# A shorter substitution completed by TensorE products, and two products of the chain formed ahead of it

## The chip, the cores and the metric

The kernel runs on one core of a Trainium2 chip. The metric is the device time of one execution in microseconds. Most executions of a kernel agree to within a per cent, and each is given a state, fast or slow, by its distance from the fastest of the same kernel. Where two kernels are compared, the executions alternate on the same chip.

## The reference

The delta rule is run as a recurrence over 768 positions for 4 batches and 8 heads of size 48. A Fourier mixing block and an MLP with float64 weights follow (code shortened).

```python
def _attn_ref(q, k, v, beta):                       # B, H, S, D = 4, 8, 768, 48
    k_n = k / (np.linalg.norm(k, axis=-1, keepdims=True) + 1e-06)
    state = np.zeros((B, H, D, D))
    for t in range(S):
        y[:, :, t] = einsum('bhd,bhde->bhe', q[:, :, t], state)
        v_old = einsum('bhde,bhd->bhe', state, k_n[:, :, t])
        state = state + beta_t * einsum('bhd,bhe->bhde', k_n[:, :, t], v[:, :, t] - v_old)
def _moe_ref(x, w_ch1, w_ch2):                      # x: 4 x 768 x 384; w: 384 x 1536, 1536 x 384
    mixed = real(fft(fft(x, axis=1), axis=2))
    u = x + mixed
    un = (u - mean(u)) / sqrt(var(u) + 1e-06)
    return u + maximum(un @ w_ch1, 0) @ w_ch2
```

## The kernel before

The recurrence is worked in chunks of 64 positions (12 per batch). Each chunk needs the inverse T of a triangular 64x64 matrix. Six groups of eight chunks each form these inverses. A chunk's matrix is split into quarters of 32: VectorE inverts the two diagonal ones of all heads at once by substitution, and TensorE completes the inverse with the products `pj`.

```python
def mm(o, lhsT, rhs, start, stop=True):
    nc.tensor.matmul(o, lhsT=lhsT, rhs=rhs, start=start, stop=stop, skip_group_check=True)

def invert(g):                                        # W = 32, QT = 4
    A = grams.pop(g)
    X = wk.tile([128, W, W], F32, tag="X", name="X")
    nc.vector.transpose(X..., A[:, :, :, 0]...)
    # ... norms, scaling by beta, mask Y on GpSimd ...
    for j in range(1, W - 1):                         # 30 steps, two VectorE operations each
        n = W - 1 - j
        t = A...[:, 0:j, 0, 0:n]
        nc.vector.tensor_tensor(t, X[:, j:j + 1, j + 1:]..., X[:, 0:j, j:j + 1]..., op=ALU.mult)
        nc.vector.tensor_tensor(X[:, 0:j, j + 1:], X[:, 0:j, j + 1:], t, op=ALU.add)
        yield
    # ...
    Z = wk.tile([128, 2 * QT, 4, W], F32, tag="X", name="Z")   # shares its buffer with X
    nc.vector.transpose(Z..., Y...)
    nc.vector.transpose(A[:, :, :, 0]..., Y...)
    for lh in range(2):                               # half groups
        for step in range(2):
            pj = ps_pair("pj", "pair")...
            # ... 32 products of 32x32 (c, u, hh) into pj, then 4 ScalarE copies into A, wt ...
            yield

def chain(m):                                         # one chunk of one batch, in series
    # pk: 8 products of the keys KQT with the state
    nc.vector.tensor_tensor(R, V4[:, c], pk, op=ALU.subtract)
    # pu: 8 products of R with wt (that is T)
    nc.scalar.activation(U, pu, ACT.Copy)
    # pS: 8 products of kp with U; VectorE adds them to the state
    later.append(outputs(...))                        # py: read by ScalarE into x

# order of the program (shortened)
run(keys(0)); run(keys(1))
first = invert(0)
advance(first, 4)
run(both(first, seq(keys(2, 3), queries(0, 1))))
scaled(0)
pre = both(invert(1), queries(2, 3))
for m in range(STEPS):
    # chain steps, between which pre is advanced, and behind pre the weights' conversion:
    # if m < 2 * QT and not advance(pre): advance(side)
    # from batch 1 on the MLP of the batch before runs beside the chain
```

An fp32 product counts as two passes of TensorE in the trace, each with a weight load of its own.

## Time and profile before

| | before |
|---|---|
| median of 4 executions | 830.9 us (828.5 to 840.1) |
| span of the profiled one | 832.2 us |
| TensorE (PE) busy | 740.3 us, 8024 passes |
| VectorE (DVE) busy | 397.8 us |
| ScalarE (ACT) busy | 286.4 us |
| first transposes of the MLP of batch 0 | 198.7 us |

The slices, the busy time by stretch and the timeline of before stand in the prediction below.

### The profile page before, as it was taken

To read this page: it belongs to the slowest core of one execution; us is meant where nothing else is said; L and a number is where in the kernel's file an instruction comes from. 1 tells how busy PE (TensorE), PEld (TensorE's weight loads), DVE (VectorE), ACT (ScalarE), POOL (GpSimd) and SP (SyncE) were. 2 spreads that over 40 slices of the span, in tenths; PEclk is the share of its full clock that TensorE was granted. 3 is DMA by queue.
4 is the path that set the end of the run, shared out by engine and by line. 5 is a ranking of instruction groups with operands and counts; after the bars stand their busy time and mean duration, and the time that the engine had idled before them with its cause. 6 is when DMAs were issued, how large, how long until landed. Compare 5 with 4: busy or idle time off the path is not lost.

```text
span 832.2 us, 18790 instructions
## 1 busy us (share of the span) xinstructions
PE 740.3 (89%) x8024; PEld 549.2 (66%) x8024; DVE 397.8 (48%) x1036; ACT 286.4 (34%) x667; POOL 45.8 (6%) x67
## 2 busy tenths in 40 slices
PE   4768777795999987899999899999899989999997
PEld 3537666674767665675766766766667667676784
DVE  5986959859931148951169313499110124210000
ACT  5725268541272142451431632511511112030120
POOL 3000000011000000010000001000000010000000
PEclk9995955587999998969999799999699999999999
DMA  7542326510111121001111001001000000000000
GB/s 159 123 96 44 61 48 219 151 25 6 25 35 23 35 41 27 14 11 35 29 19 45 2 11 30 1 2 39 2 1 20 2 20 1 9 10 20 9 10 19
DMA packets 84051, 30.81 MB, mean 37 GB/s; under 512 B 79248, under 2 KB 80784, under 8 KB 83968
## 3 DMA queue, kind: packets, MB, share of 16 engines
q1 hardware_dynamic: 80880, 26.63, 14.3%
q0 software_dynamic: 912, 2.59, 0.9%
q8 instruction: 63, 1.03, 0.5%
q10 hardware_dynamic: 2176, 0.39, 0.3%
q14 instruction: 20, 0.16, 0.1%
HBM read 24.87 MB, written 4.72 MB: 36 GB/s over the span
## 4 chain that ended last, share of the span: by engine, by line
PE 64%; DVE 16%; ACT 10%; issue 3%; DMA 3%; SPq 2%; POOL 1%; POOLq 0%; DVEq 0%; ACTq 0%
PE ph L124 20%; PE po L124 19%; PE pc L124 6%; PE py L124 5%; PE pg L124 3%; DVE X L465 3%; PE pf L124 3%; DVE A L463 3%; PE pj L124 2%; PE pb L124 2%; PE pt L127 2%; ACT A L407 2%; SPq L156 1%; ACT wt L497 1%; ACT wt L500 1%
## 5 line engine op out<-in xcount | busy, mean ns | idle before, releaser
L124 PE MATMUL ph<-unT,w 128*128 128x256 f32 x864 | 221.7, 405 | 6.2 <-ACT hT L723 2.9
L124 PE MATMUL po<-w,hT 128*128 128x384 f32 x576 | 200.3, 495 | 0.0
L124 PEld LDWEIGHTS ph<-unT,w 128*128 128x128 f32 x864 | 164.0, 198 | 37.2 <-ACT hT L723 6.1
L124 PEld LDWEIGHTS po<-w,hT 128*128 128x128 f32 x576 | 105.1, 190 | 65.3 <-issue 0.5
L723 ACT ACTIVATE hT<-ph 128x256 f32<-128x256 f32 x144 | 55.0, 383 | 207.9 <-PE ph L124 207.6
L563 DVE TENSOR_TENSOR st<-st,pc 48x192 f32<-48x192 f32 x88 | 30.9, 351 | 96.3 <-PE pc L124 62.7
L736 DVE TENSOR_TENSOR x<-x,po 128x384 f32<-128x384 f32 x24 | 13.3, 554 | 126.6 <-PE po L124 126.5
L546 ACT ACTIVATE U<-pc 128x192 f32<-128x192 f32 x48 | 15.8, 330 | 120.9 <-PE pc L124 111.8
L124 PE MATMUL pc<-R,wt 64*64 64x48 f32 x768 | 41.6, 246 | 13.1 <-DVE R L537 7.2
L124 PEld LDWEIGHTS pc<-R,wt 64*64 64x64 f32 x768 | 33.6, 156 | 28.9 <-DVE R L537 9.1
L463 DVE TENSOR_TENSOR A<-X 128x30 f32<-128x30 f32 (+9 forms) x150 | 50.5, 337 | 3.8
L465 DVE TENSOR_TENSOR X<-X,A 128x30 f32<-128x30 f32 (+9 forms) x150 | 49.2, 328 | 3.7
L124 PE MATMUL py<-st,KQT 128*64 128x96 f32 x352 | 45.9, 280 | 0.8 <-ACT x L583 0.6
L407 ACT ACTIVATE A<-pg 32x256 f32<-32x256 f32 x108 | 36.6, 369 | 19.3 <-PE pg L124 18.7
L124 PE MATMUL pg<-KQT 48*64 48x128 f32 (+1 forms) x896 | 36.7, 311 | 6.3 <-ACT w L407 2.3
L124 PE MATMUL py<-U,LQ 64*64 64x48 f32 x768 | 40.7, 240 | 0.0
L124 PEld LDWEIGHTS pg<-KQT 48*64 48x64 f32 x896 | 28.5, 177 | 17.2 <-ACT KQT L374 4.7
L124 PEld LDWEIGHTS py<-st,KQT 128*64 128x64 f32 x352 | 35.7, 155 | 5.8 <-issue 1.9
L124 PE MATMUL pf<-stab,scr 128*128 128x128 f32 (+6 forms) x192 | 28.1, 299 | 9.1 <-DVE scr L634 9.0
L124 PEld LDWEIGHTS py<-U,LQ 64*64 64x64 f32 x768 | 34.7, 154 | 2.2 <-issue 1.2
L660 DVE TENSOR_TENSOR x<-x,pb 128x193 f32<-128x193 f32 (+1 forms) x96 | 27.1, 346 | 18.3 <-PE pb L124 18.3
L124 PEld LDWEIGHTS pf<-stab,scr 128*128 128x128 f32 (+2 forms) x192 | 25.9, 193 | 13.5 <-DVE scr L634 6.4
(127 smaller groups left out, 807.2 us busy)
## 6 DMA issues: line engine op xcount, KB each, us to landing
w<-in_moe_w_ch_dram SPq DMA_DIRECT2D x12, 768.0 KB, 4.6
qp<-in_q_dram SPq DMA_DIRECT2D x96, 48.0 KB, 2.4
V<-in_v_dram SPq DMA_DIRECT2D x96, 48.0 KB, 2.4
kp<-in_k_dram SPq DMA_DIRECT2D x88, 48.0 KB, 2.4
out_dram<-x SPq DMA_DIRECT2D x8, 192.0 KB, 1.9
out_dram<-x SPq DMA_DIRECT2D x4, 168.0 KB, 2.1
stab<-k_stab SPq DMA_DIRECT2D x1, 640.5 KB, 4.7
kp<-in_k_dram ACTq DMA_DIRECT2D x8, 48.0 KB, 3.4
```

The lines of the kernel that those rows point to most:

```text
L124: nc.tensor.matmul(o, lhsT=lhsT, rhs=rhs, start=start, stop=stop, skip_group_check=True)
L127: nc.tensor.matmul(o, lhsT=src, rhs=ident[0:src.shape[0], 0:src.shape[0]], is_transpose=True, start=start, stop=True, skip_group_check=True)
L156: engs[hh].dma_start(out=dst[64 * hh:64 * hh + CH, c, :, 0:D], in_=src[b, 4 * hh:4 * hh + 4, t0:t0 + CH, :].rearrange("h p d -> p h d"))
L407: nc.scalar.activation(ce(A[pr, ns, :, sl]), src, ACT.Copy)
L463: nc.vector.tensor_tensor(t, X[:, j:j + 1, j + 1:].broadcast_to([128, j, n]), X[:, 0:j, j:j + 1].broadcast_to([128, j, n]), op=ALU.mult)
L465: nc.vector.tensor_tensor(X[:, 0:j, j + 1:], X[:, 0:j, j + 1:], t, op=ALU.add)
L497: nc.scalar.activation(wt[r1, :, :, 0:W], Z[r1, ns], ACT.Copy)
L546: nc.scalar.activation(U, pu, ACT.Copy)
L563: nc.vector.tensor_tensor(nst[pr, :, :, e, :], st[pr, :, :, e, :], pS[pr], op=ALU.add)
L660: nc.vector.tensor_tensor(dst, dst, src, op=op)
L723: nc.scalar.activation(hT[:, fc, :], ph, ACT.Relu)
L736: nc.vector.tensor_tensor(x[:, T, :], x[:, T, :], po, op=ALU.add)
```

## The change

Three things are done for the first groups or the first batch, to get the MLP started sooner (they touch groups 0 and 1, the chain of batch 0 and the front). In groups 0 and 1 VectorE substitutes over blocks of 16 instead of 32, 14 steps instead of 30. TensorE joins the blocks by products `pe` and `pz` over all four quarters. For the first batch the chain uses T B K and T B V, formed ahead of it (`pm`, `pv`), so each step of the chain loses a product and a copy. And in the front the constants are fetched first, while the products that transpose beta move behind the first keys.

```diff
+    pack = const.tile(...); bt = ...; k0 = ...; v0 = ...        # all four fetched here, ahead of the memsets
+    nc.gpsimd.dma_start(out=pack, in_=cn["pack"].ap())
...
     def invert(g):
+        narrow = g < 2
...
-        for j in range(1, W - 1):
+        for j in range(1, (H if narrow else W) - 1):            # H = 16
+            if narrow:
+                n = H - 1 - j
+                t = ts[:, :, 0:j * n].rearrange("p h (s t) -> p h s t", t=n)
+                nc.vector.tensor_tensor(t, XB[:, :, j:j + 1, j + 1:]..., XB[:, :, 0:j, j:j + 1]..., op=ALU.mult)
+                nc.vector.tensor_tensor(XB[:, :, 0:j, j + 1:], XB[:, :, 0:j, j + 1:], t, op=ALU.add)
...
         for lh in range(2):
+            if narrow:
+                quarters = [(slice(W * i, W * i + W), c, u) for c in range(QT) for u in range(4) for i in range(4)]
+                pe = ps_one([128, QT, 4, W], "pe")
+                mm(pe..., ident, eyes[:, None, :]..., True)
+                for r, c, u in quarters:
+                    mm(pe[r, c, u], A[r, QT * lh + c, u, 0], Z[r, QT * lh + c, u], False)
+                nc.scalar.activation(E[:, lh], pe, ACT.Copy)
+                pz = ps_pair("pz", "pair")...
+                for r, c, u in quarters:
+                    mm(pz[r, 0, c, u], AD[r, QT * lh + c, u], E[r, lh, c, u], c == 0 and u == 0)
+                for r, c, u in quarters:
+                    mm(pz[r, 1, c, u], E[r, lh, c, u], AD[r, QT * lh + c, u], c == 0 and u == 0)
+                nc.scalar.activation(Z[:, ns], pz[:, 0], ACT.Copy)
+                nc.scalar.activation(A[:, ns, :, 0], pz[:, 1], ACT.Copy)
...
+    def combined(m):                       # 8 products pm into KQT, 8 products pv into the values, one copy each
...
-        pu = ...; U = ...                  # for every chunk
+        if m < NCH: U = R                  # first batch: neither products nor copy
...
     run(keys(0))
+    betas()                                # was ahead of the first keys
...
-    scaled(0)
+    combined(0); combined(1)
```

## The prediction

> **What bounds the kernel now.** I read first the busy shares in 40 slices (20.8 us each, tenths).
>
> ```profile
> PE   4768777795999987899999899999899989999997
> DVE  5986959859931148951169313499110124210000
> PEclk9995955587999998969999799999699999999999
> ```
>
> From slice 10 (about 200 us) to the end TensorE (PE) is at 9 nearly everywhere; before that VectorE (DVE) is the fuller engine. So there are two stages: a preparation, and a long stretch bound by PE. The busy time by stretch sizes them (columns: PE, weight loads, DVE, ScalarE, GpSimd busy us with counts, granted clock, DMA share, GB/s).
>
> ```profile
> 26.30:62.30 36.00, 24.14 (x296) 16.32 (x296) 31.86 (x89) 15.96 (x48) 0.00 (x0) 0.97 0.48 95
> 62.30:71.30 9.00, 6.29 (x198) 5.79 (x200) 2.51 (x2) 7.39 (x13) 1.85 (x1) 0.50 0.34 58
> 71.30:113.00 41.70, 33.56 (x730) 28.25 (x730) 36.02 (x95) 11.08 (x26) 0.00 (x0) 0.75 0.27 48
> 121.80:163.40 41.60, 30.50 (x570) 26.93 (x565) 36.82 (x92) 31.69 (x72) 0.00 (x0) 0.54 0.65 191
> 163.40:198.70 35.30, 24.02 (x244) 18.93 (x242) 26.14 (x72) 11.12 (x29) 5.64 (x8) 0.79 0.12 21
> 198.70:832.00 633.30, 599.11 (x5580) 434.77 (x5580) 244.35 (x636) 185.12 (x433) 30.38 (x41) 0.95 0.08 18
> ```
>
> The last stretch has PE busy 599 of 633 us, and its programme does not change for groups 2 to 5. So the time falls by what its start (198.7, the first transposes of the MLP of batch 0) moves forward, plus PE work taken out of it. The timeline shows what separates the stretches ahead of it.
>
> ```profile
> 60.22 2.02 DVE L472 STREAM_TRANSPOSE Z<-Y 128x1024 f32<-128x1024 f32 x1
> 62.29 1.92 PE L124 MATMUL pj<-Z,A 32*32 32x32 f32 x64 [5.69 <-DVE Z L472]
> 64.25 1.19 ACT L496 ACTIVATE A<-pj 32x512 f32<-32x512 f32 x2
> 69.25 0.63 ACT L500 ACTIVATE wt<-Z 32x512 f32<-32x512 f32 x1
> 71.30 1.94 DVE L448 STREAM_TRANSPOSE X<-w 128x1024 f32<-128x1024 f32 x1 [6.49 <-issue]
> ```
>
> Group 0's substitution ends in Z; PE and ScalarE (ACT) then finish the inverse in turns; only when the last copy has left Z is its buffer free for X of group 1. That substitution runs 71 to 113, with the chain's first steps. Then comes the conversion of the float64 weights (121.8 to 163.4), then the Fourier stage of batch 0, whose scratch is the conversion's buffer, then the MLP. By tile, the conversion is
>
> ```profile
> L288 ACT ACTIVATE wtmp<-w x24: 532/550/566, 17.9 to 160.7; 128x384 int32<-128x384 uint32 x24
> L306 DVE SCALAR_TENSOR_TENSOR wtmp<-w,wtmp x24: 540/551/559, 19.3 to 162.0; 128x384 int32<-128x384 int32 x24
> L309 DVE TENSOR_SCALAR wtmp<-wtmp x24: 345/352/361, 19.8 to 162.4; 128x384 int32<-128x384 int32 x24
> L312 DVE CUSTOM_DVE_ANT_0 w<-wtmp x24: 494/551/993, 20.1 to 162.8; 128x768 uint16<-128x768 uint16 x24
> ```
>
> 21 of 24 pieces fall into those 41.6 us, in which DVE is 89% and ACT 76% busy. The conversion's end is the gate; the question is when it can begin.
>
> **What the Trainium skill says.** "VectorE: DVE Perf Modes", section "The TRN2 errata", says that operations reading SBUF pay a fixed cost per instruction. The trace agrees: 30 elements take 0.19 us, 240 take 0.41, and start to start is about 0.187 us + 1.04 ns per element. "TensorE: Matmul & The Clock Gate", Part 1, says that the array drops to half clock after an idle window of about 3.4 us and recovers after a busy one. The trace agrees: PE waits 5.69 us before 62.29, and the granted clock goes from 0.97 to 0.50. "TensorEngine Tiling (Array Packing)", "Performance Considerations", warns that tiling speeds up TensorE but not the emptying of PSUM. It agrees here: 64 passes of 32x32 take 1.92 us cold, and the two copies behind them 1.19.
>
> **The change, part by part.**
>
> Substitution. Before: steps j=1..30, two operations each of j(31-j) elements, 4960 in sum: 60 x 0.187 + 9920 x 0.00104 = 21.5 us (the page's groups L463 and L465, 50.5 + 49.2 us over five groups, agree). After: 14 steps on two blocks, 1120 elements: 28 x 0.187 + 2240 x 0.00104 = 7.6 us. **-13.9 us of DVE per group, two groups.**
>
> Added products. Per half group (four of them): an identity over 512 columns, 64 products (pe), a copy E, 128 products (pz), and two copies. This trace counts two passes per fp32 matmul: pj's 32 count as 64. That is 30 ns a pass cold, 17.6 at full clock (64 passes in 1.13 us later). The new ones walk over four array positions instead of two; products with the four-position order (pc from U, 16 in 0.40 us warm, 0.57 cold, against 0.67 and 1.09 for the two-position pc from R) are quicker, so I choose 17.5 ns: pe 2.2 us, pz 4.5, identity 0.9 (two passes at the 0.9 ns a column of po). ACT copies of 512 columns take 0.6. Serial: 2.2 + 0.7 + 4.5 + 1.2 = 8.6 us, the identity lying ahead. With the second half partly overlapped: **+14 to 15 us of PE/ACT path per group.**
>
> Front. Constants are fetched before GpSimd's memsets and the beta products go behind the first keys. First key products before: 11.45. The keys landed at 6.4, but ACT's squares and table loads hold its first copy until 10.0 instead of 12.2: **-2 us.**
>
> Chain, batch 0. Twelve times 8 products R by wt and a copy U (0.33 us) leave the path, together some 1.4 us of each 4.5 us step; 16 products and copies of about 0.38 and 0.33 us come beside it, on ACT and PE, which are filling up.
>
> Now the sum, along the compiled order of the instructions, whose positions I followed:
> - X of group 0 at 24 instead of 26.35. To Z: 1.9 + 0.9 + 1.2 + 10.3 (substitution with ten small norm operations) + 1.2 + 1.0 (scaling V, now ahead of Z) + 2.0 = 18.7 (before 35.9): Z at 42.7.
> - First half of the inverse: pe to 45, E 45.8, pz 50.4, Z and A 51.7, pj, copy, pj, copy 57.7. Second half: E 58.3, pz 62.9, Z and A 64.2, four wt copies 66.7. Only then X of group 1: 66.8, **4.5 us earlier**, where DVE alone would have given 19.
> - First chain step, U at 72.6, as before (72.5): the second half's last copies stand before it on ACT.
> - Group 1: 1.9 + 1.2 + 7.6 + 1.2 + 2.0, with two chain steps and masks between: Z at 85 (before 111 to 113).
> - Its inverse, with four more chain steps between: 29 us, end about 115 (before 130).
> - Conversion: behind that end in ACT's order. Before it began beside it, at 121.8; now about 116, with 22 pieces left and not 21, and with more chain steps among them: DVE 22 x 1.32 (start to start) = 29 us, 16 state updates x 0.38, nine subtractions, two masks and more, 15 in sum: 44 us against 41.6. **End about 160, 3 us earlier.** The loads also hold this pace: 768 KB land in 4.6 us and conversion takes 3.8, with two buffers.
> - Fourier stage: 35 us as before. By then steps 15 and part of 16 of the chain are done, which before lie in the PE-bound stretch: 3 to 4 us of PE less there.
>
> Gain: 3 + 4 = 7 us, **829.2 - 7 = 822 us**.
>
> **Rivals.**
> A. DVE is the bound throughout, and the removed 28 us plus 2 at the front arrive: about 800. For it: DVE 86 to 89% busy in three stretches. Against: the Z buffer holds X of group 1 back, and the new product path must be gone through four times in series.
> B. PE becomes the bound: if the 32x32 passes run at 30 ns, each half group costs 1.6 + 3.3 us more, 20 us in all, and the conversion ends near 175 to 180: 835 to 845. For it: clock 0.50 in these stretches before. Against: the dense new products should wake the clock, and four positions overlap.
> C. Loads hide it: the conversion's pace is set by its two buffers whatever DVE does, and only its start counts. That is in my sum.
>
> **Range and chances.** Four series stages of 7 us estimated to a fifth, and a conversion start known to about 6 us, give +-9; with A's tail 806 to 838. Faster by over 2% (under 812.7) needs 17 us: 0.24. Slower by over 2%: B in full, 0.08. Within: 0.68.
>
> **What would show it.** In the changed profile: X of group 1 near 67 and its Z near 85 (right), or X at 55 or earlier (A). Mean of a pe or pz pass 17 to 18 ns (right) or 30 (B). Granted clock over 0.7 between 43 and 70. First bulk conversion at 116 and last near 160; first ptr at 195. If conversion ends before 145, I have oversized the product path or its serial part; if the stretch from the first ptr to the end shortens by over 10 us, I have missed something in it. PE idle before pz or pj, waiting for ACT, would show that copies and not products carry the added path.

## More of the kernel before

One more line of its page will matter, from the part on DMA queues (queue, kind: packets, MB, share of 16 engines). It is the queue that brings the instructions themselves:

```profile
q8 instruction: 63, 1.03, 0.5%
```

## The result, and the profile after

The changed kernel took a median of 864.9 us (862.7 to 870.4, 4 executions) against 830.9 us. The ratio is 1.040, with a 95% interval of 1.030 to 1.050. A ratio here and below is the mean time of one kernel's fast executions over that of the other's of the same rounds, so it is not quite the ratio of the medians quoted. The prediction was 822 us, with 838 as the upper end of its range.

The 40 slices of the page after (21.6 us each, in tenths):

```profile
PE   4588879788599998789999999999899998999997
DVE  5924603886993115875208731468511013400000
PEclk9975866757699998895999979999979999999999
```

VectorE was relieved as intended. Counted from 0, its slices 2, 3, 5 and 6 are at 0 to 4, where slices 1 to 7 of before were all at 5 to 9. Yet PE gets to its long run of 7 to 9 only in slice 11 (238 us), where before it was slice 10 (208 us). The busy time by stretch says where the time went (columns as in the prediction: PE, weight loads, DVE, ACT, GpSimd, granted clock, DMA share, GB/s):

```profile
28.50:44.70 16.20, 9.03 (x161) 6.84 (x153) 15.56 (x49) 11.86 (x35) 0.52 (x1) 1.00 0.53 121
44.70:78.20 33.50, 27.07 (x1088) 21.61 (x1086) 5.55 (x6) 12.80 (x24) 1.58 (x2) 0.64 0.22 41
...
98.10:137.80 39.70, 30.42 (x1245) 25.32 (x1244) 7.25 (x14) 16.10 (x30) 0.00 (x0) 0.72 0.13 24
145.00:196.00 51.00, 42.65 (x801) 35.42 (x799) 43.90 (x111) 33.90 (x81) 1.44 (x1) 0.67 0.66 179
196.00:230.60 34.60, 24.24 (x252) 19.28 (x252) 25.61 (x71) 10.60 (x28) 3.78 (x7) 0.80 0.21 37
230.60:865.00 634.40, 598.76 (x5484) 434.71 (x5484) 242.20 (x630) 184.36 (x431) 30.38 (x41) 0.94 0.07 17
```

- X to Z of group 0 shrank from 36.0 to 16.2 us: the substitution became shorter as worked out.
- The products that follow until X of group 1 take 33.5 us, where before it was 9.0. The same part of group 1 takes 39.7 us. In both VectorE is nearly idle (5.6 and 7.3 us).
- The conversion of the weights takes 51 us instead of 41.6. The Fourier stage (34.6) and the rest (634.4 against 633.3) are as before.

So nearly all of the 33 us (32 of them) lie ahead of the MLP: its first transposes start at 230.6 instead of 198.7. Inside the product stretch, the timeline of PE shows what it does (start, duration, passes, idle time before and what ended it):

```profile
47.01 1.39 PE L125 MATMUL pe<-Z,A 32*32 32x32 f32 x128
...
49.15 0.96 PE L125 MATMUL pz<-E,w 32*32 32x32 f32 x75
51.37 0.62 PE L125 MATMUL pz<-E,w 32*32 32x32 f32 x51 [1.27 <-issue]
...
51.85 0.79 PE L125 MATMUL pz<-w,E 32*32 32x32 f32 x73
55.10 0.96 PE L125 MATMUL pz<-w,E 32*32 32x32 f32 x53 [2.46 <-issue]
```

The array is fast: 128 passes of `pe` in 1.39 us, 10 to 11 ns a pass. But `pz` comes in pieces, and between them PE stands still for 1.3 and 2.5 us waiting for nothing that the trace shows ("issue"). The piece at 51.37 and the one at 55.10 are 3.7 us apart, with 128 passes from the one start to the other. Over the window from 40 to 160 us the view of PE's waits sums this up (us in total, times, longest):

```profile
PE pz L125 <- issue: 12.2, 7, 2.5
```

And the queue that carries instructions moved more, in the page after:

```profile
q8 instruction: 77, 1.26, 0.6%
```

Before it was 63 packets and 1.03 MB, so a packet is 16.4 KB. The 8024 passes of before, at two instructions a pass (weight load and matmul), make that 64 bytes an instruction, so a packet holds 256 instructions, or 128 passes. The change adds 1736 passes, which makes 0.22 MB. That is the 0.23 MB seen, within the rounding to whole packets.

### The profile page after: what moved, and what is told of

Same layout as the page of the kernel before. It is cut to its first block, busy times and chain, and to the rows that moved or that the text cites.

```text
span 865.1 us, 22233 instructions
## 1 busy us (share of the span) xinstructions
PE 772.8 (89%) x9760; PEld 575.8 (67%) x9760; DVE 375.6 (43%) x972; ACT 297.7 (34%) x693; POOL 46.8 (5%) x71
## 3 DMA queue, kind: packets, MB, share of 16 engines
q1 hardware_dynamic: 80880, 26.63, 13.5%
## 4 chain that ended last, share of the span: by engine, by line
PE 70%; DVE 12%; ACT 8%; issue 4%; DMA 4%; SPq 1%; POOL 0%; POOLq 0%; ACTq 0%; DVEq 0%
PE ph L125 21%; PE po L125 19%; PE py L125 6%; PE pc L125 6%; PE pg L125 3%; PE pf L125 3%; PE pj L125 3%; DMA w<-in_moe_w_ch_dram 2%; PE pt L128 2%; PE pb L125 2%; DVE X L493 2%; PE pz L125 2%; DVE A L491 1%; DVE Z L500 1%; PE pe L125 1%
## 5 line engine op out<-in xcount | busy, mean ns | idle before, releaser
L622 ACT ACTIVATE U<-pc 128x192 f32<-128x192 f32 x36 | 11.9, 331 | 105.9 <-PE pc L125 105.3
L125 PEld LDWEIGHTS pg<-KQT 48*64 48x64 f32 x896 | 28.4, 177 | 25.1 <-ACT KQT L381 16.4
L125 PE MATMUL py<-U,LQ 64*64 64x48 f32 x768 | 43.1, 245 | 0.0
L493 DVE TENSOR_TENSOR X<-X,A 128x30 f32<-128x30 f32 (+14 forms) x120 | 40.6, 339 | 3.2
L417 DVE TENSOR_TENSOR LQ<-pg,pack 128x512 f32<-128x512 f32 x24 | 16.4, 685 | 58.8 <-PE pg L125 32.6
L491 DVE TENSOR_TENSOR A<-X 128x30 f32<-128x30 f32 (+14 forms) x120 | 39.6, 330 | 3.2
L125 PEld LDWEIGHTS py<-st,KQT 128*64 128x64 f32 x352 | 34.6, 151 | 8.3 <-ACT x L659 3.8
L125 PEld LDWEIGHTS pc<-R,wt 64*64 64x64 f32 x576 | 24.0, 151 | 21.0 <-issue 8.1
L125 PE MATMUL pc<-R,wt 64*64 64x48 f32 x576 | 29.8, 240 | 7.0 <-ACT wt L548 4.1
```

The source lines that it names most:

```text
L417: nc.vector.tensor_tensor(ce(LQ[:, 2 * c2:2 * c2 + 2]), pv[:, :, :, 1 - a0], mb[:, None, None, :].broadcast_to([128, 2, 4, CH]), op=ALU.mult)
L491: nc.vector.tensor_tensor(t, X[:, j:j + 1, j + 1:].broadcast_to([128, j, n]), X[:, 0:j, j:j + 1].broadcast_to([128, j, n]), op=ALU.mult)
```

## The theory and its rivals

- **T1, supply.** PE gets its instructions in blocks of 128 passes, and a block takes some 3.7 us to arrive. Long runs of small passes therefore cost about 29 ns each, although the array needs 10.
- **R2**, the products T B K and T B V ahead of the chain cost most. **R3**, the front costs most.
- **R4**, the turns between PE and ScalarE's copies carry it. **R5**, the array itself at half clock carries it.

The skill has a page for T1, which I found only after the result. "Runtime: NRT & Kernel Launch", section "Instruction fetch mechanics", says that instructions come in blocks of 16 KiB, 256 instructions, by the sequencer's own DMA queue. It adds that the cost of crossing a boundary is "mostly hidden". The trace agrees with the block size and, with 1.3 to 2.5 us of standstill at these boundaries, not with the last point.

## The experiments

All ran on chips of the same kind, each beside executions of the kernel before: 829.0 us in the first two sets, 832.9, 834.0 and 834.2 in the later ones. Results were correct unless noted. The table is a summary of 13 kernels; the others follow in the text. PE busy is that of the profiled execution. "Rest" is its span less PE busy.

| kernel | what it is | median us (range) | ratio to before [95%] | PE busy | rest |
|---|---|---|---|---|---|
| before | | 830.9 | 1 | 740.3 | 91.9 |
| after | the change | 864.9 (862.7–870.4) | 1.040 [1.030, 1.050] | 772.8 | 92.3 |
| e_inv_only | inverse alone | 857.5 (848.8–862.1) | 1.027 [1.021, 1.033] | 767.2 | 91.7 |
| e_comb_only | T B K, T B V alone | 845.7 (833.3–849.1) | 1.012 [1.002, 1.022] | 749.0 | 98.4 |
| e_front_only | front alone | 840.3 (838.1–841.5) | 1.007 [1.001, 1.014] | 743.9 | 95.8 |
| e_oldfront | all but the front | 860.5 (845.7–860.9) | none | 768.3 | 90.8 |
| e_onepass | pe, pz in one pass | 848.2 (846.8–849.4) | 1.023 [1.019, 1.027] | 757.4 | 87.4 |
| e_dvetr | half of pz by VectorE | 844.3 (828.2–849.6) | none | 756.8 | 85.6 |
| e_dvetr_again | the same | 844.0 (841.5–846.9) | 1.012 [1.008, 1.015] | 757.9 | 87.3 |
| e_inv_dvetr | inverse alone, so | 845.2 (839.2–849.7) | 1.014 [1.007, 1.020] | 761.8 | 86.2 |
| e_subst_only | no added products (wrong) | 823.2 (817.0–823.8) | 0.985 [0.981, 0.990] | 736.5 | 85.6 |
| e_before_fill | before + 64 large products | 873.7 (872.6–879.7) | 1.048 [1.045, 1.051] | 790.5 | 87.5 |
| e_least_pe | inverse alone, 128 passes | 832.3 (826.6–833.5) | 0.996 [0.992, 1.001] | 749.2 | 82.6 |

("None": three of the four executions were labelled slow against one fast one.)

### Parts alone: e_inv_only, e_comb_only, e_front_only, e_oldfront

```diff
# e_inv_only: front of before, and no T B K, T B V
-        if m < NCH:            U = R ...
+        if False:              U = R ...
-    combined(0); combined(1)
+    scaled(0)
# e_comb_only: front of before, and the long substitution
-        narrow = g < 2
+        narrow = False
# e_oldfront: the change with pack, bt, k0, v0 fetched and betas() placed as before
# e_front_only: the change with both of the first two edits, but its own front
```

> Only the shorter substitution with its PE products (groups 0 and 1); the order of the front and the first batch's chain are those of before. Theory T1: the added products cost the time, because PE is supplied with instructions no faster than about 29 ns a pass over long runs, though the array does these passes in about 10 ns. Then the issue waits in pz stay (about 12 us, pieces of pz again about 3.7 us apart) and the time is 848 to 862 against 830 of before. Rival R2, that the products formed ahead of the chain (T B K, T B V) cost most: 826 to 838 here. Rival R3, that the new order of the front costs most: below 840 here.

The time was 857.5 us, with PE waiting for issue in `pz` for 10.1 us. This is what T1 expects; R2 and R3 fall as main causes. It shows that the inverse carries the loss, not yet why.

> Only T B K and T B V formed ahead of the chain for the first batch; substitution over the whole 32 and the front as before. T1: no long run of 32x32 passes is added, so the time is within 1% of before, 824 to 836. R2 (these products and their copies on ScalarE cost most): 845 to 860. R3 (front): as before, 824 to 836.

The time was 845.7 us, with a wide range (833.3 to 849.1). T1 missed: these products do cost something by themselves, 1.2% by the fast executions and up to 2% by the median. R2's band was met here, but the inverse alone costs more. Beside the inverse the runs do not agree: e_dvetr with front and these products (844.0 to 844.3) is no slower than e_inv_dvetr without both (845.2), but the change is 1.3% or 11 us slower than e_inv_only (ratios 1.040 and 1.027), which lacks both. The profile fell on a slow execution, so I explain nothing from it.

> Only the order of the front (constants fetched ahead of the first memsets, beta products behind the first keys); substitution and chain as before. R3: the front costs 3 us or more: 832 to 836, X of group 0 at 28 to 29 us instead of 26.3. If the front costs nothing: 827 to 831.

The front alone costs some 6 to 7 us: 840.3 against 832.9, ratio 1.007 with an interval of 1.0005 to 1.014. That is above both bands. X of group 0 begins at 28.47 us, as R3 said, 2 us later than before; the first transposes of the MLP begin 4 us later (202.7) and the stretch behind them takes 637.0 us instead of 633.5. In the changed kernel the first products of the keys (`pg`) do begin sooner, at 11.0 us instead of 12.6. But the 48 passes that transpose beta (2.74 us from 15.85) stand amid the first keys, whose next transposes start only at 18.52. That this is the reason was not tested apart.

> The changed kernel with the order of the front put back (constants behind the first memsets, beta products ahead of the first keys). T1 with a small front share: 2 to 5 us less than the changed kernel, so 859 to 863, X of group 0 at 26 to 27 instead of 28.6. R3 (the front costs most of it): below 850.

Three executions near 860.5 and one at 845.7 allow no ratio. 4 us less by the median and an X of group 0 at 26.3 us fit a small share of the front, but the spread leaves it open.

### The supply: e_onepass, e_dvetr, e_dvetr_again, m_supply

```diff
# e_onepass: the upper halves of the same words, as bf16 (not exact, within the tolerance)
-    mm(pe[r, c, u], A[r, QT * lh + c, u, 0], Z[r, QT * lh + c, u], False)
+    mm(pe[r, c, u], hi16(A[r, QT * lh + c, u, 0]), hi16(Z[r, QT * lh + c, u]), False)      # pz likewise
# e_dvetr, e_dvetr_again: (E'AD) is the transpose of (AD'E), block by block
-    for r, c, u in quarters:
-        mm(pz[r, 1, c, u], E[r, lh, c, u], AD[r, QT * lh + c, u], c == 0 and u == 0)
-    nc.scalar.activation(A[:, ns, :, 0], pz[:, 1], ACT.Copy)
+    nc.vector.transpose(A[:, ns, :, 0]..., pz[:, 0]...)
```

> The changed kernel with the products pe and pz reading the upper 16 bits of the same words as bf16: one pass each instead of two, so 768 passes (and as many weight loads) fewer; results slightly off on purpose. T1: 768 passes at about 29 ns each no longer have to be supplied, some 20 us, less the part that lies beside other work: 840 to 850, issue waits in pz below 2 us instead of 12. Rival R4, that the turns between PE and the copies on ScalarE carry the loss: the number of turns is unchanged, so at most 5 us less: 858 to 865. Rival R5, that the cold clock carries it whatever is supplied: the passes run cold at half the array time, some 5 us less: 856 to 862, and no waits for issue.

The time was 848.2 us, 17 less than the change, in T1's band; R4 and R5 missed. The same view of PE's waits, between 40 and 160 us, now has

```profile
PE pz L125 <- issue: 0.9, 1, 0.9
```

instead of 12.2 us in seven waits. X of group 1 began at 69.5 (78.3 in the change). Of the 20 us between the two profiled spans, 15 are PE busy time (772.8 to 757.4) and 5 are rest, so this edit removes array time and waits together; m_supply below takes them apart.

> The changed kernel with the second half of pz (64 products, 128 passes per half group) replaced by a transpose of the first half on VectorE, exact: 512 passes and as many weight loads fewer in all. T1: 512 passes at 29 ns, 15 us less supply, less about 1 us of transpose per half group: 850 to 857, X of group 1 near 72, first bulk conversion near 131. R4 (turns between PE and ScalarE carry it): one ScalarE copy per half group of 0.6 us fewer, 860 to 865. R5 (cold clock at the array): 512 passes at 10 to 15 ns, 5 to 8 us, 857 to 860.

> The same kernel as e_dvetr, to see its spread: either most runs near 844 again with some near 828, or one level. If the profile falls on a run near 828, its granted clock and the stretch before the first transposes of the MLP tell where the 16 us lie; a colder stretch of PE in the run of 844 is expected.

Taking 128 of the 384 passes away per half group, exactly, gave 844 us in both sets, 20 less than the change and below T1's band of 850 to 857. By the ratios 1.040 and 1.012 it is 23 us, or 45 ns for each of 512 passes, more than the supply accounts for; one ScalarE copy per half group went too, and what the surplus is was not tested. In the second set X of group 1 began at 72.8 and the bulk conversion at 123.5. One of eight executions took 828.2 us with a granted clock of 0.927 (0.899 to 0.910 in the seven others). No profile fell on it, so what it did otherwise stays open; e_oldfront and e_comb_only also had one such execution each.

To measure the supply apart from everything, blocks of products were put behind the end of the kernel before:

```diff
+    block("mA", 512, 32, 32, False, 0)     # 512 fp32 products 32x32, 32 columns, four positions
+    block("mB", 512, 32, 8, False, 1)      # 8 columns
+    block("mC", 1024, 32, 32, True, 2)     # bf16, one pass each
+    block("mD", 128, 128, 128, False, 3)   # 128x128, 128 columns
+    ... eight weight loads of 768 KB ...
+    block("mE", 512, 32, 32, False, 4)     # as mA, beside the loads
```

> The kernel before, with five blocks of products behind its end, whose results go nowhere: mA 512 fp32 products of 32x32 with 32 columns (1024 passes), mB the same with 8 columns, mC 1024 bf16 products of 32x32 with 32 columns (1024 passes), mD 128 fp32 products of 128x128 with 128 columns (256 passes), mE as mA while eight weight loads of 768 KB run. T1 (PE is supplied with 128 passes, 16 KB of instructions, in about 3.7 us): mA, mB and mC take the same time, about 29 ns a pass or 30 us each, with waits for issue every 128 passes; mD is bound by the array. If mE is as fast as mA the supply doesn't suffer from the other transfers; if it is much slower, the supply in the changed kernel was slow because weights and keys were landing. Rival (array time, R5): mB takes a quarter to a half of mA, and no waits for issue appear.

Groups of instructions of this run (count, busy us, mean ns, idle before and its cause), then pieces of its timeline:

```profile
L861 PE MATMUL mD<-msrc 128*128 128x128 f32 x256 | 31.3, 289 | 0.0
...
L861 PE MATMUL mB<-msrc 32*32 32x8 f32 x1024 | 15.3, 197 | 14.6 <-issue 14.6
L861 PE MATMUL mE<-msrc 32*32 32x32 f32 x1024 | 14.6, 229 | 20.5 <-issue 19.8 <-DVE msrc L874 0.7
L861 PE MATMUL mA<-msrc 32*32 32x32 f32 x1024 | 14.6, 226 | 12.1 <-issue 12.1
...
L861 PE MATMUL mC<-msrc 32*32 32x32 bf16 x1024 | 10.0, 188 | 18.6 <-issue 18.6
```

```profile
843.99 1.93 PE L861 MATMUL mA<-msrc 32*32 32x32 f32 x128 [1.82 <-issue]
847.46 1.93 PE L861 MATMUL mA<-msrc 32*32 32x32 f32 x128 [1.54 <-issue]
...
872.85 1.89 PE L861 MATMUL mB<-msrc 32*32 32x8 f32 x128 [1.85 <-issue]
876.60 1.89 PE L861 MATMUL mB<-msrc 32*32 32x8 f32 x128 [1.86 <-issue]
...
901.99 1.22 PE L861 MATMUL mC<-msrc 32*32 32x32 bf16 x128 [2.25 <-issue]
905.74 1.22 PE L861 MATMUL mC<-msrc 32*32 32x32 bf16 x128 [2.52 <-issue]
...
951.59 1.93 PE L861 MATMUL mE<-msrc 32*32 32x32 f32 x128 [4.22 <-issue]
957.26 1.93 PE L861 MATMUL mE<-msrc 32*32 32x32 f32 x128 [3.73 <-issue]
```

(The blocks lie behind the end, so the time of this one execution, 983.0 us, is not compared.) Apart from the ends of the blocks every piece has 128 passes, and the pieces of mA, mB and mC follow each other after 3.5 to 4.0 us, whether a pass has 32 columns or 8 and whether it is half of an fp32 product or a whole bf16 one. That is 27 to 31 ns a pass, set by nothing but the count. From fp32 to bf16 a piece keeps PE busy for 1.22 us instead of 1.93, and the idle time grows by as much. From 32 to 8 columns the busy time hardly changes (1.93 and 1.89 us), so mB alone would not separate supply from array; mC does. The rival said that mB takes a quarter to a half of mA, and it takes the same.

The packets of the instruction queue agree: from 857 to 884 us it brings 7 packets for 7 pieces of mB, from 887 to 912 us 7 for 7 of mC (`prof m_supply --dma` with these windows). The large products of mD, 122 ns a pass, show no such wait.

While the weight loads land (to about 971 us) the pieces of mE come 4.0 to 5.7 us apart, after that 3.7: the supply shares something with the other transfers. And mE began with 170 passes in a row although PE had been in mD for 31 us, so no more than that lay ready. T1 stands as an account of the waits.

### What the saving is worth, and what PE time costs: e_subst_only, e_before_fill, e_least_pe, e_inv_dvetr

The edits that relieve the supply took away 17 to 20 us and left some 15. The question was whether the shorter substitution was worth its length at all.

```diff
# e_subst_only: inverse alone, the products pe and pz left out (results wrong on purpose)
-                pe = ...; 64 products; copy E; pz: 128 products; copies Z, A
+                nc.scalar.activation(A[:, ns, :, 0], AD[:, ns], ACT.Copy)
# e_before_fill: the kernel before, with large products of zero weights between those of pj
                             mm(pj[r1, hh, c, u], *ops, c == 0 and u == 0)
+                            if g < 2 and u == 3:
+                                fill(pj[r1, hh])          # 512 columns, bf16, 32 rows, adds zeros
# e_inv_dvetr: e_inv_only with the edit of e_dvetr; e_least_pe: that, and pe, pz as in e_onepass
```

> Only the shorter substitution over two blocks of 16, without the products pe and pz and their copies E and Z (results wrong on purpose: the inverse lacks its off-diagonal part; one copy into A stays); front and chain as before. If the VectorE time saved is worth what the stretches suggest (28 us of substitution on the path, rival A of the prediction): 800 to 808. If it is worth little because PE, ScalarE and the order of the conversion hold the preparation: 820 to 829. The difference to e_inv_only (857.5) is then the whole price of the added products.

The relative error is 0.072, as meant. The time is 823.2 us against 834.0, ratio 0.985. So with nothing added, 26 us less substitution on VectorE is worth 11 to 12 us. That is the smaller of the two bands, though X of group 1 began 19 us sooner than before, as the timeline of VectorE shows:

```profile
51.94 1.94 DVE L457 STREAM_TRANSPOSE X<-w 128x1024 f32<-128x1024 f32 x1 [6.62 <-ACT wt L533]
```

The conversion then began at 99.1 us and ended near 151.5, so it took 11 us longer than before. Half of the lead was lost there, and the MLP began at 186.8, 12 us sooner than before.

The difference to e_inv_only, by ratios 1.027 less 0.985, is 4.2% or 35 us. This is the price of the added products, with their copies. In the profiled spans it is 36.8 us: 30.7 of PE busy time and 6.1 of rest. `pe` and `pz` keep PE busy for 28.9 us in e_inv_only, the identity included, and PE waits for issue in `pz` for another 10.1. So the supply is one part of the price, and the time of the passes themselves the larger one.

> The kernel before with 64 large bf16 products of zero weights (512 columns, 0.33 us each at full clock) put between the small products pj of groups 0 and 1: 21 us of PE work more, some 30 if at half clock, results unchanged. If PE time counts one for one in the preparation: 848 to 862. If PE has room there (it is busy 70 to 80% of those stretches): 830 to 840.

The group of these fillers in the trace:

```profile
L124 PE MATMUL pj<-stab,gz 128*32 128x512 bf16 x64 | 38.9, 608 | 0.0
```

They took 38.9 us, since they ran at half clock (0.61 us each and not 0.33), and the time rose by 40 us. So PE time in the path of the inverse counts about one for one, although PE has idle time in these stretches. (In the profiled execution, the slowest of five, PE busy rose by 50 us, so other passes became 11 us slower.) The table agrees roughly: over all its kernels the rest beside PE busy stays between 83 and 98 us, while PE busy itself moves by 54. The band I gave was too low because I had the size of a filler wrong.

> Only the shorter substitution, with half of pz by a VectorE transpose; front and first batch's chain as before. From e_inv_only (857.5) the same step as from the changed kernel to e_dvetr, 15 to 20 us: 838 to 843 if the parts add up. If the products ahead of the chain were what stood in the way, it would reach before or less: 820 to 832.

> The shorter substitution alone with the least PE work tried: half of pz by a VectorE transpose, and pe and pz from the upper 16 bits as bf16, one pass each; front and chain as before (not exact, within the tolerance). If PE time and the supply carry the loss, PE busy time is about 10 us over that of before, and the time 834 to 840, below e_inv_dvetr (845). If something else holds the rest, 842 to 848.

e_inv_dvetr took 845.2 us, 2 above its band; e_least_pe took 832.3, 2 below its band, with 8.9 us more PE busy time than before, as expected. With e_inv_only, three kernels now differ mainly in the passes of `pe` and `pz` per half group: 384, 256, 128. (The last two also have e_dvetr's transpose in place of a copy, and the last has bf16 passes.) Their ratios to before are 1.027, 1.014, 0.996. That is some 1.5% or 12.6 us per 128 passes, or for the four half groups 25 ns a pass. It is close to the rate of the supply, not to the 10 ns of the array (15 at half clock). With 128 passes `pz` no longer waits for issue and the loss is gone, but what is left of the saving is inside the interval. The trace shows where it went: the MLP begins at 191.9 us, 7 sooner than before, and the stretch behind it takes 639.9 us instead of 633.5. Why it grows was not tested.

### Whether the cold clock behind the stalls costs: e_dvetr_warm, e_inv_dvetr_warm

```diff
                 for i, (r, c, u) in enumerate(quarters):
                     mm(pe[r, c, u], ...)                 # and pz
+                    if i % 8 == 7:
+                        fill(pe)                         # one bf16 product of zero weights, 512 columns
```

> The kernel e_dvetr (half of pz by a VectorE transpose) with one large bf16 product of zero weights (128x128, 512 columns) behind every 8 of the small products of pe and pz: 16 per half group, two instructions each, adding zeros to the same bank. If the stalls of the supply cost a second time, because the clock drops to 0.50 while PE waits for instructions, then the fillers lie inside the waits, keep the granted clock over 0.8 between 44 and 72 us and between 98 and 120 us, and the time falls from 844 to 832 to 840. If the cold clock behind the stalls costs nothing: 844 to 850[...].

> e_inv_dvetr with the fillers. If the cold clock behind the stalls costs: 5 to 10 us below e_inv_dvetr, 828 to 836, and so about the time of before. If not: the same as e_inv_dvetr or up to 4 us above.

e_dvetr_warm took 862.3 us (855.5 to 863.0; ratio 1.032), 18 more than without. e_inv_dvetr_warm took 870.8 (870.2 to 873.5; ratio 1.046). In e_dvetr_warm the granted clock was 1.00 between 60 and 80 us (0.50 without), as wanted. But the fillers took 26 us of PE together and did not fit into the waits: 16 passes and a filler follow each other in 0.585 us, where the supply needs 16 x 28 = 450 ns. Both missed the band. A warm clock may have given back 26 less 18, some 8 us, but that is argued. In e_inv_dvetr_warm the fillers took 32.6 us, since many ran at 0.61 us, and the time rose by 26; the same sum gives 7. The price of the cold clock is not settled.

```profile
54.15 0.40 PE L125 MATMUL pe<-stab,gz 128*128 128x512 bf16 x1
54.48 0.33 PE L125 MATMUL pe<-Z,A 32*32 32x32 f32 x16
54.74 0.40 PE L125 MATMUL pe<-stab,gz 128*128 128x512 bf16 x1
```

### Whether the idle VectorE could be used: e_early, e_before_early

```diff
-    run(both(first, seq(keys(2, 3), queries(0, 1))))
+    run(both(first, seq(keys(2, 3), queries(0, 1)), late(side, 14, 10)))   # conversion beside the products
-    pre = both(invert(1), queries(2, 3))
+    pre = both(invert(1), queries(2, 3), late(side, 20, 10))
# e_before_early: the same two edits to the kernel before, with 30 and 36 in place of 14 and 20
```

> The changed kernel with 10 of the 22 late weight pieces converted beside the product path of the two inverses, where VectorE is idle (DVE busy 3 to 4 of 20 us there). If the time freed on VectorE is lost because the conversion stands behind the inverse in the program's order, 12 pieces remain after the inverse instead of 22: some 15 to 22 us less than the changed kernel, 843 to 850. Rival: ScalarE or the weight loads have no room beside the products, and the product path gets longer by as much: 860 to 868.

> The kernel before with the same 10 pieces moved ahead in the same way, as a control: there VectorE is at 86% in the stretches concerned, so the pieces only push the substitution back: 824 to 836. If it gains as much as the changed kernel does (12 us or more), the order of the conversion has nothing to do with the VectorE time freed.

e_early took 862.3 us (858.6 to 864.8; ratio 1.039 against 1.040 of the change): no gain. Its last conversion began at 167.7 us instead of 193.5, and the MLP at 218.9 instead of 230.6. But from there to the end it took 641.8 us instead of 634.4, so most of the gain was given back. Its PE busy time (771.4 us) is that of the change. The control e_before_early lost 11 us (842.3; ratio 1.014) where I expected nothing, so moving the pieces has a price of its own, and the test does not separate the two. (In the control PE busy rose by as much, 11.3 us at the same number of passes, and the MLP began 10 us later.) What it does show is that a sooner start of the MLP is not by itself a sooner end.

### A version that beats both? e_least_pe_noid, e_inv_dvetr_noid

The two passes that add the identity (about 1 us each, twice per group) were replaced by an addition on VectorE while it empties `pe`.

```diff
-    mm(pe..., ident, eyes[:, None, :]..., True)
-    nc.scalar.activation(E[:, lh], pe, ACT.Copy)
+    nc.vector.tensor_tensor(E[:, lh]..., pe..., eyes[:, None, :]..., op=ALU.add)
```

> e_least_pe with the identity added by VectorE while it empties pe, instead of by two PE passes of 128x512 (0.96 us each) per half group. If PE time in this path counts one for one: 4 x 1.9 = 7.7 us less PE, so 824 to 828 against 832 of e_least_pe, and 0.5 to 1.2% below before. If the identity lay beside other work: 830 to 834.

> The exact version, the same step from e_inv_dvetr (845): 837 to 840 if one for one, so still slower than before (834); 843 to 847 if the identity lay beside other work.

They took 833.0 us (826.3 to 837.1, six executions; ratio 0.999) and 848.7 (844.9 to 851.5; ratio 1.018). The first lies in the band for an identity beside other work, the second 2 us above it. But neither shows that PE time beside other work is free: `pe` lost 7.4 and 5.1 us of PE time, while PE busy as a whole fell by 2.3 us in the first and rose by 0.7 in the second, so other passes became slower. (In e_inv_dvetr_noid the first 128 passes of `pe` took 1.93 us, in e_inv_dvetr 1.44; the granted clock on record, 1.00 from 40 to 125 us, does not agree with such durations.) In the exact version the MLP also began 5 us sooner (207.3 instead of 212.4), and the stretch behind it took 4 us longer (639.8). What the identity costs stays open. No version here beats the kernel before. e_least_pe equals it, and is not exact.

## Why the prediction was wrong, point by point

| step | predicted | before | measured |
|---|---|---|---|
| X of group 0 | 24 | 26.4 | 28.6 |
| end of Z, group 0 | 42.7 | 62.2 | 44.7 |
| last wt copies, first half group | 57.7 | | 65.4 |
| X of group 1 | 66.8 | 71.3 | 78.3 |
| end of Z, group 1 | 85 | 113.0 | 98.1 |
| bulk conversion | 116 to 160 | 121.8 to 163.4 | 145.1 to 196 |
| first transposes of the MLP | 195 | 198.7 | 230.6 |
| from there to the end | 627 | 633.5 | 634.5 |

- **Substitution: right.** The groups of the narrow steps (28 operations each) are 6.8 and 6.6 us for both inverses together, 6.7 us per inverse. The long substitution takes (50.5 + 49.2)/5 = 19.9. The saving is 13.2 us per group; 13.9 was predicted. X to Z took 16.2 us, against 18.7 (the terms that the prediction lists for it add to 18.5).
- **Added products: this step failed.** It reads "so I choose 17.5 ns: pe 2.2 us, pz 4.5". The 384 passes of a half group were put at 6.7 us. If all came at the 28 ns of the supply they would need 10.8 us, 4.1 more, four times: 16 us as an estimate. In the trace `pz` took 6.9, 5.4, 6.0 and 7.8 us from first to last, 26.1 against the 18 forecast, of which PE waited 12.2 for issue and was busy 13.9; `pe` took 10.8 against 8.8, with other passes between. So the two were short by 10 us as measured. e_onepass, which takes 192 of 384 passes away, gained 17. I had taken a rate of the array, a slow one even for it (`pz` kept PE busy for 13.5 ns a pass), and did not ask how fast instructions arrive.
- **Where the 43 us of the miss lie** (865 and not 822), from the table and the stretches: X of group 0 +4.6, X to Z of group 0 -2.6, the product stretches of the two groups +9.5 and +9.7, X to Z of group 1 +1.6, from the end of the inverse to the bulk conversion +6.3, the conversion +7, the Fourier stage 0, the last stretch +7.5. The product stretches are the largest part; `pe` and `pz` are half of that, the work that stands between them in PE's and ScalarE's order the other half.
- **Rival B** named 30 ns a pass and 835 to 845 us. It had the size right and the reason wrong: not the array at half clock, since mA to mC have the same rate at different array times. Its band was still 20 us too low; some 8 of them are the front, which it left as a gain.
- **Front: wrong in sign.** -2 us was predicted; the front alone costs 6 to 7 us. The first keys did come sooner, but the lead was gone by X of group 0; the moved beta products stand between, and whether they are the reason was not tested.
- **Chain.** The prediction had it about even in the preparation and 3 to 4 us less PE work in the last stretch. Beside the inverse the runs do not settle its cost; alone it costs 1 to 2%; and the last stretch did not get shorter.
- **"PE idle before pz or pj, waiting for ACT" did not show.** PE waited for issue there, which my list of signs lacked.
- **Conversion and the rule of the finish line.** It began 29 us later than predicted, as the inverse of group 1 ended at 137.8 instead of 115, and it took 7 us longer. e_subst_only shows how little of VectorE's time reaches the end even if nothing is added: 26 us of work saved gave 11 to 12. The prediction had set 28 us saved against 28 to 30 added; the runs give 12 and 35. So of the two, the worth of the saving was missed by more than the price. "The time falls by what its start moves forward" held for the change itself to 1 us but failed in e_early and e_least_pe, where the last stretch took 6 to 8 us longer than before.
- **Rival A**, about 800 us, is ruled out by e_subst_only: even without products the saving ends at 823.

Worked as shares of 830 us: the saving -12, the added products +35 (of which some 25 go with 256 of the 384 passes), the front +6, the products ahead of the chain +10 alone and unsettled beside the inverse. The sum without the last is 29, against 33 measured. The 4 us between lie within the intervals.

**Open:** why three of the kernels have rare executions 12 to 16 us faster than the rest; what a cold clock behind the stalls costs; what the supply shares with the weight loads; what the products ahead of the chain cost beside the inverse; and why the last stretch grows in some kernels whose MLP starts sooner.

## What to carry to other kernels

Before moving work to TensorE, count the instructions and not only the array time: a run of several hundred small passes came at about 28 ns a pass here, whatever a pass did, so fewer and larger passes, a bf16 pass instead of two, or a transpose on an idle engine were worth more here than a faster pass. Look for waits for issue that recur every 128 passes with a steady period. And test what a saving is worth by itself, by leaving out the part that pays for it (even with wrong results), before building that part.

## What the Trainium skill lacked or had wrong

- "Runtime: NRT & Kernel Launch", section "Instruction fetch mechanics", calls the crossing of a 16 KiB boundary "mostly hidden". In runs of small passes it was not: 256 instructions took 3.5 to 4.0 us to arrive (mA to mC), 4.0 to 5.7 us beside weight loads (mE). PE waited 12.2 us for them in the changed kernel.
- "TensorE: Matmul & The Clock Gate", Part 1, gives about 25 ns as the least distance of two matmuls. The 128 passes of `pe` over four positions took 1.39 us, about 10 ns each as the trace counts passes, and 128 whole bf16 products of mC 1.22 us. The floor that was met was the supply, 27 to 31 ns. Its rule that the array recovers its clock once busy did not predict e_before_fill either: there PE was busy for 56.2 of the 65 us from 135 to 200, at a granted clock of 0.50. I found no statement of what work counts as busy, and no run here isolates it.
